# Two-layer attention and gMLP on one Trainium2 core: turning the mixer's operand two tiles ahead and preparing w_out inside the mixer

## The chip, the cores and the metric

The kernel runs on one core of a Trainium2 chip. A core has five engines with queues of their own, each worked through in order: TensorE (PE, whose weight loads have their own row, PEld), VectorE (DVE), ScalarE (ACT), GpSimd (POOL) and SyncE (SP), which here issues every DMA. The metric is the device time of one execution in microseconds, median of several runs.

## The reference

Two layers of attention, each followed by a gated mixer, on 2048 rows of 640 values:

```
x = x + A(layernorm(x));  x = x + B(layernorm(x))      # twice

def B(x, w_in, w_sp, b_sp, w_out):                     # w_in 640 x 1728, w_sp 2048 x 2048, w_out 864 x 640
    z = gelu(x @ w_in)
    z1, z2 = z[..., :864], layernorm(z[..., 864:])
    g = w_sp @ z2 + b_sp[:, None]
    return (z1 * g) @ w_out
```

A is a segmented attention with 32 heads and a compressive memory; the change does not touch it. Every matrix product is done in float16 with each operand split into a high and a low half (x = h + l), in three products: hh, hl and lh.

## The kernel before, in words

Each layer has three stages.

**Attention** (`phase1a`) ends with the projections of row tiles 0 to 11 (x1 = x + o @ wo, stored to DRAM). Tiles 12 to 15 are left to the next stage.

**The mixer** (`phase1b`) goes over the 16 row tiles of 128 rows in the order ts = 0..3, 12..15, 4..11. For each it loads x1 (for tiles 12 to 15 it makes x1 from the attention output `o`, L372 and L375), normalizes it (L303 to L312), splits it into two float16 halves `xnhl` (`split_t`: L318 on ACT, L319 on DVE) and turns it by a transposing DMA into `th` (L320), the stationary operand. Then PE makes the two halves of z = x @ w_in (L395, 30 matmuls each): z2 first, then z1, each followed by a gelu on ACT (L401, L408). z2 is normalized and seven combinations of it are kept as `zb` (L448, L449, L453); z1 goes to DRAM (L409). The half z2 has two accumulators (`zp1`), the half z1 has one (`zp0`). The loop is one tile ahead: in iteration i it loads tile i+2, turns the operand of tile i+1 and multiplies tile i. `th` has two buffers. In the first layer each iteration also advances `other_scales` for w_out by one step (seven loads of 128 rows, a largest value of each, then the scale: L271 to L291), and iterations 7 and 9 store the split w_in (L201, four stores of 1080 KB).

**The spatial stage** (first layer: `phase2f`, second: `phase2s`) multiplies w_sp by z2 in a Strassen-like scheme: eight pairs of row tiles, seven products of 24 matmuls a pair (P1 to P7, L796), whose operands are sums of quarters of w_sp (S1 to S4, made by POOL L781, DVE L784 and L790 and ACT L787 from turned quarters, L760, L764, L773). The gated rows are multiplied by w_out (L876). `SEVEN` is the written order of a pair's steps, with lags in pairs. `PREPARED` lists steps of the first pairs that are put into the mixer: `rows1.0:1` is step rows1 of pair 0, to be issued after the gelu and the normalization of the mixer's tile 1; names without a number come right at the mixer's end.

w_out (`g.wu`, 864 x 640 float32, seven pieces of 128 rows) is split by `staged()` in the first pairs: a piece is loaded to a staging tile (L824), then `split_scaled` makes its two halves on ACT (L90) and DVE (L91), straight into the place that w_in's second half had. After pair 2, `keep()` stores the halves to DRAM (L201, L203: two stores of 960 KB and two of 120 KB); the second layer brings them back from there with `bring()`.

PE's order in the mixer, and that of all engines in the spatial stage, is the program's. The order of the other engines in the mixer is made by a planner, which simulates the engines and hands an instruction to an engine when its inputs are there in that simulation; `issue_after` holds a step until another instruction. Once planned, each queue's order is fixed, and an engine whose next instruction waits does nothing else.

Of the kernel before, what the change touches and what calls it, by code (L numbers as in the profile page):

```python
# [9 lines left out]
F32 = mybir.dt.float32  # L10
# [75 lines left out]
def split_scaled(g, h, l, st, c):  # L86

    nc = g.nc
    iv = g.iv[:st.shape[0], c:c + 1]
    nc.scalar.activation(h, st, AF.Identity, scale=iv)  # L90
    return nc.vector.scalar_tensor_tensor(l, st, iv, h, ALU.mult, ALU.subtract).ins  # L91
# [244 lines left out]
def phase1b(g, o_d, x, x1_d, z1_d, put, after):  # L336
    nc, tc = g.nc, g.tc
    first = not g.wu.made
    with ExitStack() as ctx:
        pool = lambda n, b, **k: ctx.enter_context(tc.tile_pool(name=n, bufs=b, reuse_waits="tile", **k))  # L340
        right = lambda n, b: pool(n, b, side="right")
        if first:
            pool("bp", 1).tile([128, 6 * 1024], F32, name="bp")
            wm = pool("bm", 2)
        pe2, pe1, p2, p1, px2, px1 = right("be2", 2), right("be1", 1), right("b2", 2), right("b1", 1), right("bx2", 2), right("bx1", 3)
        pz1, py, pz0 = pool("bz1", 2, space=PSUM), pool("by", 1, space=PSUM), pool("bz0", 1, space=PSUM)
        ctx.enter_context(tc.manual_schedule(engines=ENGINES))
        wi = [(w.h, w.l) for w in g.wi]
        woh, wol = g.wo.h, g.wo.l

        def load(t):
            if t < NWO:
                x1 = pe2.tile([128, D], F32, tag="x1", name="x1")
                nc.sync.dma_start(x1, x1_d[t])
                return (x1,)
            xt = px2.tile([128, D], F32, tag="xt", name="xt")
            nc.sync.dma_start(xt, x[t])
            o = px1.tile([128, 2, KD, 128], F16, tag="o", name="o")
            d = o_d[t // 4][(t % 4) * 128:(t % 4 + 1) * 128]
            nc.sync.dma_start(o.rearrange("p i k c -> p (i k) c"), d.rearrange("p i c -> p (i c)"), transpose=True)  # L360
            return xt, o[:, 0], o[:, 1]

        def attn_out(t, *a):
            if t < NWO:
                x1 = a[0]
            else:
                xt, oh, ol = a
                yp = py.tile([128, 2, 512], F32, tag="yp", name="yp")
                for k in range(KD):
                    for j, (a, b) in enumerate(((oh, woh), (oh, wol), (ol, woh))):  # L370
                        for n in range(2):
                            nc.tensor.matmul(yp[:, n, :320], a[:, k, :], b[:, k, n * 320:(n + 1) * 320],  # L372
                                             start=(k == 0 and j == 0), stop=(k == KD - 1 and j == 2))
                x1 = pe2.tile([128, D], F32, tag="x1", name="x1")
                nc.vector.scalar_tensor_tensor(x1.rearrange("p (n c) -> p n c", n=2), yp[:, :, :320], g.yw,  # L375
                                               xt.rearrange("p (n c) -> p n c", n=2), ALU.mult, ALU.add)
                nc.sync.dma_start(x1_d[t], x1)
            xn = x1 if t < NWO else xt
            layernorm(g, x1, xn, D, 2, XS)
            return xn  # L380

        def xn_t(xn):
            th = pe2.tile([128, 2, KD, 128], F16, tag="th", name="th")
            hl = pe1.tile([128, 2, D], F16, tag="xnhl", name="xnhl")
            split_t(g, hl, th, xn)
            return th[:, 0], th[:, 1]

        def w_in_half(i, th, tl):
            zp = (pz0, pz1)[i].tile([128, 2, 512], F32, tag=f"zp{i}", name=f"zp{i}")
            wh, wl = wi[i]  # L390
            for k in range(KD):
                for j, (a, b) in enumerate(((th, wh), (th, wl), (tl, wh))):
                    for n in range(2):
                        c = n * FHH
                        nc.tensor.matmul(zp[:, n, :FHH], a[:, k, :], b[:, k, c:c + FHH],  # L395
                                         start=(k == 0 and j == 0), stop=(k == KD - 1 and j == 2))
            return zp

        def z2_half(t, zp):
            z2 = p1.tile([128, FH], F32, tag=f"z2{t % 2}", name="z2")  # L400
            i = nc.scalar.activation(z2.rearrange("p (n c) -> p n c", n=2), zp[:, :, :FHH], AF.Gelu_apprx_tanh, scale=g.zi[1])  # L401
            j = layernorm(g, z2, z2, FH, 2, ZB)
            put(t, z2, p1)
            return i.ins, j.ins

        def z1_half(t, zp):
            z1 = p2.tile([128, FH], F32, tag="z1", name="z1")
            nc.scalar.activation(z1.rearrange("p (n c) -> p n c", n=2), zp[:, :, :FHH], AF.Gelu_apprx_tanh, scale=g.zi[0])  # L408
            return nc.sync.dma_start(z1_d[t], z1).ins  # L409


        g.mark = {}
        ts = [*range(4), *range(NWO, NT), *range(4, NWO)]
        with after(-9):
            a = load(ts[0])
            xn = attn_out(ts[0], *a)
            a = load(ts[1])
            th = xn_t(xn)
        more = other_scales(g, wm, (g.wu,), 6, 0, 0) if first else iter(())
        for i, t in enumerate(ts):  # L420
            late = lambda: ExitStack() if i else after(0)
            b = load(ts[i + 2]) if i + 2 < NT else None
            if i + 1 < NT:
                with late():
                    th1 = xn_t(attn_out(ts[i + 1], *a))
            a = b
            last = z2_half(t, w_in_half(1, *th))
            g.mark[i] = last
            sent = z1_half(t, w_in_half(0, *th))
            th = th1  # L430
            with tc.issue_after(last[1]), tc.issue_after(sent):
                if first and i in (7, 9):
                    g.wi[i == 7].keep()
                for _ in range(1 + (i == 7)):
                    next(more, None)


# [274 lines left out]
""".split()  # L712

PREPARED = """
rows1.0:1 rows0.0:1 max1.0:2 sm1.0:2 max0.0:4 sm0.0:4 hi11.0:5 lo11.0:6 hi22.0:6 lo22.0:6 T11.0:8 T22.0:8 hi21.0:8
lo21.0:8 T21.0:9 rows1.1:9 hi12.0:9 bk22.0:10 bk11.0:10 st11.0:10 lo12.0:10 max1.1:10 rows0.1:11 st22.0:11 bk21.0:12
mS1.0:12 mS3.0:12 mS2.0:13 H2.0:13 max0.1:14 L2.0:14 sm1.1:14 sm0.1:14 H1.0 L1.0 T12.0 hi11.1 st12.0 lo11.1 hi22.1
""".split()


def phase2f(g, w_sp, x1_d, z1_d, zb, out, nxt, rest):
# [93 lines left out]
            held.enter_context(tc.issue_after(i))  # L815
        return held

    def staged():

        w = g.wu  # L820
        for k in range(w.nk):
            n = min(128, w.dram.shape[0] - 128 * k)
            st = nxt.e2.tile([128, D], F32, tag="xt", name="wst")[:n] if k % 2 else nxt.e1.tile([128, D], F32, tag="xh", name="wst")[:n]
            nc.sync.dma_start(st, w.dram[k * 128:k * 128 + n])  # L824
            yield
            split_scaled(g, w.h[:n, k], w.l[:n, k], st, w.c)

    live = {}

    def new(nm, pool, tag, shape, dt=F32):  # L830
# [52 lines left out]
    def item(n, k):  # L883

        a, b = n[:-1], n[-1]
        if a in ("rows", "max", "sm"):
            t = 2 * k + int(b)
            if a == "rows":
                raw[t] = pr.tile([128, S], F32, tag="wr", name="wr")
# [81 lines left out]
    for n, k in ahead:  # L971
        with tc.issue_after(g.mark[NT - 1][n[0] in "Ll"]):
            item(n, k)
    wu = staged()
    for w in range(NP):
        for n, lag in order:
            k = w - lag
            if not 0 <= k < NP or (n, k) in early:
                continue
            with tc.issue_after(g.parted) if w == 0 else ExitStack():  # L980
                item(n, k)
            if (w, n) in ((0, "P1"), (0, "P3"), (0, "P4"), (0, "P5"), (0, "P6"), (0, "P7"), (1, "P1"), (1, "P2")):
                next(wu, None)
            if w + 1 == NP and n in ("P4", "P5", "P6"):
                a = "qkv"[int(n[1]) - 4]
                nc.sync.dma_start(g.wf[a], g.wkept[a])
                if n == "P5":
                    nxt.turned()
        if w == 2:
            g.wu.keep()  # L990
    for w in range(NP, NP + 3):
        for n, lag in order:
            k = w - lag
# [127 lines left out]
class Attention:  # L1121
# [45 lines left out]
    @contextmanager  # L1167
    def after(self, t):

        with self.tc.high_priority(offset=HP2), ExitStack() as held:  # L1170
            for i in self.marks[min(int(1.25 * t) + self.T, max(self.marks))]:
                held.enter_context(self.tc.issue_after(i))
            yield

    def next(self, f):

        if self.now is None:
            f()
        elif self.half is not None:
            self.half.append(f)  # L1180
        else:
            self.post(1, f)
# [798 lines left out]
```

## Time and profile before

| What | Value |
|---|---|
| median of 3 runs | 2202.07 us (2201.21 to 2203.7) |
| the profiled execution | 2203.07 us, of it 2201.3 us span |
| first mixer, from its first z matmul to the first product of the spatial stage | 593.5 to 797.3 us |
| first spatial stage until the next attention's projections begin to mix in | 797.3 to 1134.8 us |
| second mixer | 1669.3 to 1861.0 us |
| PE busy over the span | 2072.4 us (94%) |
| DVE busy | 1624.7 us (74%) |
| ACT, POOL busy | 1218.1 us (55%), 1083.2 us (49%) |

A row of the windows view gives, for a stretch of time, the busy time of each engine with its instructions, then TensorE's granted clock, the mean share of the 16 DMA engines that were busy and what they moved. A row of the waits view says who waited for whom, the total, how many times and the longest. A row of the timeline gives start, duration, engine, line and, in brackets, the idle time before it and what ended it. In the chain of waits a row is a piece of the path that set the end: start, length, what.

### The profile page before, as it was taken

How to read it: one execution, taken by the hardware profiler on the slowest of the kernel's cores; microseconds unless marked ns; L12 is line 12 of the kernel's file. 1: busy time of each engine (PE TensorE's matmuls, PEld its weight loads, DVE VectorE, ACT ScalarE, POOL GpSimd, SP SyncE). 2: the span in 40 equal slices, each digit the busy share in tenths (PEclk: the TensorE clock that was granted, in tenths of full speed). 3: DMA queues.
4: the chain of work that ended last, by engine and by line, in shares of the span. 5: the costliest groups of instructions: out<-in, count | busy, mean ns of one | idle time of the engine just before them, and what ended most of it. 6: DMA issues, size and time to landing. Idle time of an engine off the chain costs nothing.

```text
span 2201.3 us, 48857 instructions
## 1 busy us (share of the span) xinstructions
PE 2072.4 (94%) x19725; PEld 1250.6 (57%) x19725; DVE 1624.7 (74%) x2952; ACT 1218.1 (55%) x1490; POOL 1083.2 (49%) x704
## 2 busy tenths in 40 slices
PE   4889899999899998999999999999999999999999
PEld 2455565666555454555555556566665555555555
DVE  8678888787777788899845887877775686565464
ACT  3499888788633343332323998888874244323221
POOL 2298988888422442344330987788873233000000
PEclk9999999999999999999999999999999999999999
DMA  5626635456757658999676344344567334988885
GB/s 168 184 65 207 157 89 141 109 136 148 208 137 188 170 149 229 236 223 243 181 227 146 95 123 105 106 124 114 138 162 196 102 101 134 276 199 208 226 206 115
DMA packets 514483, 356.16 MB, mean 162 GB/s; under 512 B 409872, under 2 KB 450704, under 8 KB 509136
## 3 DMA queue, kind: packets, MB, share of 16 engines
q1 hardware_dynamic: 514256, 353.04, 61.3%
q8 instruction: 154, 2.52, 0.5%
q14 instruction: 73, 0.60, 0.1%
HBM read 157.44 MB, written 107.43 MB: 120 GB/s over the span
## 4 chain that ended last, share of the span: by engine, by line
PE 66%; DVE 12%; ACT 8%; DMA 5%; issue 5%; POOL 3%; SPq 1%; ACTq 0%; DVEq 0%; POOLq 0%
PE zp L395 12%; PE cyp L594 4%; PE cyp L876 4%; PE vps L1384 3%; PE yps L1416 3%; PE ga L546 3%; PE gb L546 3%; PE pv L1673 3%; ACT P L1620 3%; PE qps L1440 3%; PE mp L1613 3%; PE b L796 3%; PE a L796 2%; PE kps L1440 2%; ACT PHL L1638 2%
## 5 line engine op out<-in xcount | busy, mean ns | idle before, releaser
L1639 POOL TENSOR_TENSOR PHL<-P,PHL 128x1024 f16<-128x1024 f32 x310 | 658.8, 2133 | 184.2 <-ACT PHL L1638 136.6
L1620 ACT ACTIVATE P<-es,sc 128x1024 f32<-128x1024 f32 x320 | 356.1, 1113 | 89.7 <-PE es L1584 87.2
L1630 DVE TENSOR_REDUCE mx<-mp 128x2 f32<-128x1024 f32 (+2 forms) x384 | 321.2, 863 | 85.3 <-PE mp L1584 84.0
L1638 ACT CAST PHL<-P 128x1024 f16<-128x1024 f32 x320 | 333.5, 1042 | 6.3
L395 PEld LDWEIGHTS <-th 128*128 128x128 f16 x1920 | 187.7, 98 | 174.0 <-DMA th<-xnhl 11.8
L796 PEld LDWEIGHTS <-wt 128*128 128x128 f16 x1344 | 131.7, 98 | 124.4 <-DVE wt L790 8.9
L1673 PEld LDWEIGHTS <-PHL 128*128 128x128 f16 x5120 | 167.1, 96 | 56.8 <-DVE oat L1694 19.0
L306 POOL TENSOR_TENSOR lnrs<-lnve,mhalf 128x1 f32<-128x1 f32 x78 | 48.9, 635 | 303.0 <-DVE lnve L305 251.3
L546 PEld LDWEIGHTS <-wt 128*128 128x128 f16 x1344 | 131.2, 98 | 113.0 <-DMA wt<-turned 0.4
L395 PE MATMUL zp<-wi,th 128*128 128x432 f16 x960 | 182.2, 349 | 9.8 <-DMA th<-xnhl 9.7
L1673 PE MATMUL pv<-vs,PHL 128*128 128x41 f16 x5120 | 172.9, 182 | 19.4 <-DVE oat L1694 15.5
L395 PE MATMUL zp<-w,th 128*128 128x432 f16 x960 | 180.4, 347 | 0.0
L1440 PEld LDWEIGHTS <-zb 128*128 128x128 f16 x1200 | 103.1, 99 | 103.0 <-issue 8.5
L781 POOL TENSOR_TENSOR f<-wt 128x1024 f32<-128x1024 f16 x32 | 82.3, 2578 | 139.0 <-DVE wt L790 117.8
L1613 PEld LDWEIGHTS <-qk 64*128 64x128 f16 (+1 forms) x1728 | 65.7, 94 | 127.7 <-issue 94.3
L1613 PE MATMUL mp<-qk 60*128 60x512 f16 (+3 forms) x864 | 108.5, 305 | 18.1 <-DVE mx L1630 12.5
L1416 PE MATMUL yps<-wo,o 128*128 128x320 f16 x720 | 121.0, 305 | 0.0
L1613 PE MATMUL es<-qk 64*128 64x256 f16 (+3 forms) x864 | 106.1, 298 | 9.5 <-ACT P L1620 7.5
L1384 PE MATMUL vps<-zb,w 128*128 128x320 f16 x480 | 83.9, 307 | 4.8 <-DVE phl L1481 4.8
L876 PE MATMUL cyp<-w,ut 128*128 128x320 f16 (+1 forms) x630 | 88.1, 300 | 0.0
L1627 DVE TENSOR_REDUCE mx<-mp 128x4 f32<-128x1024 f32 x64 | 77.8, 1215 | 10.9 <-PE mp L1584 10.8
L1440 PE MATMUL qps<-w,zb 128*128 128x512 f16 x300 | 83.0, 380 | 0.0
(311 smaller groups left out, 4165.6 us busy)
## 6 DMA issues: line engine op xcount, KB each, us to landing
wr<-in_B_w_sp_dram SPq DMA_DIRECT2D x32, 1024.0 KB
qk<-st SPq DMA_DIRECT2D x216, 120.0 KB
z<-z SPq DMA_DIRECT2D x32, 432.0 KB
cz<-z SPq DMA_DIRECT2D x32, 432.0 KB
turned<-wt SPq DMA_DIRECT2D x24, 512.0 KB
wt<-turned SPq DMA_DIRECT2D x24, 512.0 KB
st<-qhl SPq DMA_DIRECT2D x40, 256.0 KB
st<-khl SPq DMA_DIRECT2D x40, 256.0 KB
```

The lines of the kernel that those rows point to most:

```text
L395: nc.tensor.matmul(zp[:, n, :FHH], a[:, k, :], b[:, k, c:c + FHH], start=(k == 0 and j == 0), stop=(k == KD - 1 and j == 2))
L546: nc.tensor.matmul(o[:, :FHH], wt[:, x, m, :], zb[b][:, y, m, :], start=start and i == j == 0, stop=i == NP - 1 and j == 2, skip_group_che ...
L796: nc.tensor.matmul(o[:, :FHH], w[:, x, m, :], zb[b][:, y, m, :], start=start and i == j == 0, stop=i == NP - 1 and j == 2, skip_group_chec ...
L876: nc.tensor.matmul(yp[n][:, :320], a[:kn[k], k, :], b[:kn[k], k, n * 320:(n + 1) * 320], start=(k == 0 and j == 0), stop=(k == KO - 1 and ...
L1416: nc.tensor.matmul(ps, a[:, k, :], b[:, k, c], start=(i == 0), stop=(i == 14))
L1440: nc.tensor.matmul(ps, a[:, k, c], b[:, k, :], start=(i == 0), stop=(i == 14))
L1613: nc.tensor.matmul(out[:, h, o:o + w], a[r, ac], b[r, bc], start=o == 0, stop=False, skip_group_check=True)
L1620: self.last_of["ACT"] = nc.scalar.activation(self.Pf[t], es, AF.Exp, scale=g.esc).ins
L1630: self.last_of["DVE"] = nc.vector.tensor_reduce(mx[:, e, :, i], mp[:, :, o:o + w], AX.X, ALU.max).ins
L1638: nc.scalar.copy(hl[:, 0], P)
L1639: (nc.gpsimd if t < self.T - self.TAIL or t % 2 == 0 else nc.vector).tensor_tensor(hl[:, 1], P, hl[:, 0], ALU.subtract)
L1673: nc.tensor.matmul(pv[:, i, h, 0:PVC - 1], self.P[u][:, x, h, o:o + 128], v[:, j, h0 + h, :], start=first and h == x == 0 and (u, o, i, j) ...
```

## The change

- Both mixers are two tiles ahead. Iteration i loads tile i+3, makes and turns the operand of tile i+2, and multiplies tile i. `th` gets a pool of its own with three buffers (the pool beside x1 had two), 2560 bytes more per partition on the right side of the memory, so that the pools behind it move. The output product of tiles 12 to 15 (L372) comes one tile earlier in PE's order.
- In the first layer's mixer the scale of w_out is advanced by two steps in each of iterations 0 to 3 and by one after (before: one, and two in iteration 7).
- The seven pieces of w_out become steps of `PREPARED`: `wl` loads a piece into one staging tile, `ws` splits it into one pair tile `whl`, `wk` stores the two halves to DRAM (14 stores of 160 KB, the last two of 120 KB). They are placed after mixer tiles 7 to 15. Staging tile and pair tile have one buffer each.
- In pair 0 of the first spatial stage four loads bring w_out's halves from DRAM (`bring()`, at P2, P3, P5, P6); the splitting there and the store after pair 2 are gone.
- Some other steps of `PREPARED` move: lo11.0, max0.1, sm1.1 and sm0.1 by one tile earlier, hi11.1 and lo11.1 from the mixer's end to its tile 14.

```diff
-        pe2, pe1, p2, p1, px2, px1 = right("be2", 2), ...
+        pt3, pe2, pe1, p2, p1, px2, px1 = right("bt3", 3), right("be2", 2), ...
...
-            th = pe2.tile([128, 2, KD, 128], F16, tag="th", name="th")
+            th = pt3.tile([128, 2, KD, 128], F16, tag="th", name="th")
...
             a = load(ts[1])
-            th = xn_t(xn)
+            ths = [xn_t(xn)]
         more = other_scales(g, wm, (g.wu,), 6, 0, 0) if first else iter(())
+        with after(0):
+            b = load(ts[2])
+            ths.append(xn_t(attn_out(ts[1], *a)))
+        a = b
         for i, t in enumerate(ts):
-            late = lambda: ExitStack() if i else after(0)
-            b = load(ts[i + 2]) if i + 2 < NT else None
-            if i + 1 < NT:
-                with late():
-                    th1 = xn_t(attn_out(ts[i + 1], *a))
-            a = b
+            if i + 2 < NT:
+                b = load(ts[i + 3]) if i + 3 < NT else None
+                ths.append(xn_t(attn_out(ts[i + 2], *a)))
+                a = b
+            th = ths.pop(0)
...
-                for _ in range(1 + (i == 7)):
+                for _ in range(1 + (i < 4)):
                     next(more, None)
...
-rows1.0:1 rows0.0:1 max1.0:2 sm1.0:2 max0.0:4 sm0.0:4 hi11.0:5 lo11.0:6 hi22.0:6 lo22.0:6 T11.0:8 T22.0:8 hi21.0:8
-lo21.0:8 T21.0:9 rows1.1:9 hi12.0:9 bk22.0:10 bk11.0:10 st11.0:10 lo12.0:10 max1.1:10 rows0.1:11 st22.0:11 bk21.0:12
-mS1.0:12 mS3.0:12 mS2.0:13 H2.0:13 max0.1:14 L2.0:14 sm1.1:14 sm0.1:14 H1.0 L1.0 T12.0 hi11.1 st12.0 lo11.1 hi22.1
+rows1.0:1 rows0.0:1 max1.0:2 sm1.0:2 max0.0:4 sm0.0:4 hi11.0:5 lo11.0:5 hi22.0:6 lo22.0:6 wl0.0:7 T11.0:8 T22.0:8 ws0.0:8
+hi21.0:8 lo21.0:8 wk0.0:9 wl1.0:9 T21.0:9 rows1.1:9 hi12.0:9 lo12.0:10 ws1.0:9 bk22.0:10 bk11.0:10 st11.0:10 wk1.0:10
+wl2.0:10 ws2.0:10 max1.1:10 rows0.1:11 st22.0:11 wk2.0:11 wl3.0:11 ws3.0:11 bk21.0:12 mS1.0:12 mS3.0:12 wk3.0:12 wl4.0:12
+ws4.0:12 mS2.0:13 H2.0:13 max0.1:13 sm1.1:13 sm0.1:13 wk4.0:13 wl5.0:13 ws5.0:13 L2.0:14 hi11.1:14 lo11.1:14 wk5.0:14
+wl6.0:14 ws6.0:14 wk6.0:15 H1.0 L1.0 T12.0 st12.0 hi22.1
...
+        w = g.wu
+        if a == "wl":
+            n = min(128, w.dram.shape[0] - 128 * int(b))
+            piece[:] = [nxt.e2.tile([128, D], F32, tag="xt", name="wst")[:n], nxt.e1.tile([128, 2, D], F16, tag="xh", name="whl")[:n]]
+            nc.sync.dma_start(piece[0], w.dram[128 * int(b):128 * int(b) + n])
+        elif a == "ws":
+            split_scaled(g, piece[1][:, 0], piece[1][:, 1], piece[0], w.c)
+        elif a == "wk":
+            for i in range(2):
+                nc.sync.dma_start(w.kept[i][:piece[1].shape[0], int(b)], piece[1][:, i])
...
-    wu = staged()
+    wu = g.wu.bring()
+    g.wu.made = True
...
-            if (w, n) in ((0, "P1"), (0, "P3"), (0, "P4"), (0, "P5"), (0, "P6"), (0, "P7"), (1, "P1"), (1, "P2")):
-                next(wu, None)
+            if w == 0 and n in ("P2", "P3", "P5", "P6"):
+                next(wu)
...
-        if w == 2:
-            g.wu.keep()
```

More of the change, by code (lines that the diff above doesn't have):

```diff
@@ L344, in phase1b @@
             wm = pool("bm", 2)
-        pe2, pe1, p2, p1, px2, px1 = right("be2", 2), right("be1", 1), right("b2", 2), right("b1", 1), right("bx2", 2), right("bx1", 3)
+        pt3, pe2, pe1, p2, p1, px2, px1 = right("bt3", 3), right("be2", 2), right("be1", 1), right("b2", 2), right("b1", 1), right("bx2", 2), right("bx1", 3)
         pz1, py, pz0 = pool("bz1", 2, space=PSUM), pool("by", 1, space=PSUM), pool("bz0", 1, space=PSUM)
@@ L429, in phase1b @@
             sent = z1_half(t, w_in_half(0, *th))
-            th = th1
             with tc.issue_after(last[1]), tc.issue_after(sent):
@@ L816, in behind @@
         return held
[L818 to L826, printed above, removed]
+    piece = []
     live = {}
@@ L885, in item @@
         a, b = n[:-1], n[-1]
-        if a in ("rows", "max", "sm"):
+        w = g.wu
[8 more added lines that the diff above has]
+                nc.sync.dma_start(w.kept[i][:piece[1].shape[0], int(b)], piece[1][:, i])
+        elif a in ("rows", "max", "sm"):
             t = 2 * k + int(b)
```

## The prediction

> **What bounds the kernel now.** I read the page first (PE is busy 94% of the span), then the windows around both mixers, then who waited for whom on PE there, then PE's timeline and the chain of waits for each gap, and last DVE's groups. The windows, with PE, PEld, DVE, ACT, POOL, then clock, DMA share and GB/s:
>
> ```profile
> 616.19:698.37 82.18, 82.17 (x480) 46.84 (x480) 61.32 (x111) 28.21 (x41) 21.56 (x24) 1.00 0.48 128
> 698.37:797.26 98.89, 89.82 (x480) 47.19 (x481) 74.96 (x133) 39.01 (x56) 40.10 (x34) 0.98 0.69 169
> 797.26:841.94 44.68, 35.73 (x196) 18.87 (x194) 41.46 (x48) 16.53 (x23) 14.81 (x8) 0.93 0.78 220
> 841.94:884.00 42.06, 42.06 (x242) 24.19 (x243) 36.46 (x54) 13.41 (x16) 15.12 (x7) 0.96 0.83 211
> ```
>
> PE is full in the first half of the first mixer and again from the second pair on. Between, from 698 to 842, it lacks 9.1 us in the mixer and 9.0 us in the first pair. PE's waits from 560 to 860 name the releasers:
>
> ```profile
> PE zp L395 <- DMA th<-xnhl: 9.7, 5, 4.9
> PE c L796 <- DVE wt L790: 7.1, 1, 7.1
> PE c L796 <- DVE u L803: 1.8, 1, 1.8
> ```
>
> PE's timeline has the places; the row at 933 is in a later pair:
>
> ```profile
> 616.19 5.65 PE L395 MATMUL zp<-wi,th 128*128 128x432 f16 x30 [0.59 <-DMA th<-xnhl]
> 700.77 5.65 PE L395 MATMUL zp<-wi,th 128*128 128x432 f16 x30 [2.40 <-DMA th<-xnhl]
> 713.05 5.65 PE L395 MATMUL zp<-wi,th 128*128 128x432 f16 x30 [1.16 <-DMA th<-xnhl]
> 729.10 7.33 PE L395 MATMUL zp<-wi,th 128*128 128x432 f16 x30 [4.92 <-DMA th<-xnhl]
> 775.35 5.65 PE L395 MATMUL zp<-wi,th 128*128 128x432 f16 x30 [0.60 <-DMA th<-xnhl]
> 834.28 0.52 PE L796 MATMUL c<-zb,wt 128*128 128x432 f16 x2 [1.82 <-DVE u L803]
> 841.94 5.99 PE L796 MATMUL c<-zb,wt 128*128 128x432 f16 x22 [7.13 <-DVE wt L790]
> 933.32 4.19 PE L796 MATMUL b<-zb,wt 128*128 128x432 f16 x22 [0.87 <-DVE wt L790]
> ```
>
> So there are two troubles: operands that land late, and DVE, which is late with S1 of the second pair. The gaps also cost clock: 30 matmuls take 7.33 us behind the 4.92 us gap instead of 5.65, and 22 take 5.99 behind the 7.13 us gap where 22 take 4.19 behind 0.87. That is 1.7 and 1.8 us more.
>
> In the second mixer the chain shows ten tiles without a gap. One tile takes 10.95 us, in both:
>
> ```profile
> 1751.49 109.50 PE zp L395 x600
> 631.39 10.95 PE zp L395 x60
> ```
>
> **The operand two tiles ahead.** How long the turning takes, in the chain of waits:
>
> ```profile
> 696.44 4.28 DMA th<-xnhl
> 703.75 9.26 DMA th<-xnhl
> 716.34 12.71 DMA th<-xnhl
> 770.45 4.86 DMA th<-xnhl
> ```
>
> With two buffers an operand can be written only once the tile before the running one is done, so it has one tile, 10.95 us, for normalizing, splitting, waiting in SP's queue and landing. A landing of 12.71 alone is longer. With three buffers it has 21.9 us, which leaves 9.2 us for the rest even at 12.71; DVE's part of it takes 3.2 (groups below). So I take all five waits as gone: 9.67 us (0.59 + 2.40 + 1.16 + 4.92 + 0.60) and 1.7 us of clock, 11.4 us. Bounds: nothing, if SP's order keeps the transposes where they are, and 11.4.
>
> The rest of this edit costs nothing that I see. The loads are the same, one tile earlier. In the second mixer nothing can be gained (ten tiles without a gap). Two rows of the chain and of SP's timeline, at the end of the attention:
>
> ```profile
> 598.67 6.72 DMA o<-ohl
> 605.40 3.07 SPq L360 DMA_TRANSPOSE o<-o  x2
> ```
>
> L372 moves one tile earlier: its matmuls would now start at about 616, and SP issues the first `o` at 605.4, when the attention's last store has landed. Moved pools can wait for other old tiles; the nearest row is this store of 160 KB, for which z1's first gelu waited too. That wait ends at 605.4 and is hidden today because z2 has a second accumulator; unhidden it costs at most 6.7 us, once a mixer. I take 0.
>
> **w_out in the mixer.** Two rows of the chain of waits, the first product with w_out and a load behind the four stores:
>
> ```profile
> 852.31 5.71 PE cyp L876 x42
> 922.12 8.93 DMA cz<-z
> ```
>
> Out of the first pairs go seven loads of 320 KB or less, seven L90 on ACT and seven L91 on DVE; four loads with the same 2.21 MB (864 x 640 in two float16 halves) come in, needed only by the first w_out product, now at 852 us. Out of pair 2 go the four stores, another 2.21 MB; they go into the mixer as 14. So DMA moves 2.21 MB more in all. The windows by stage:
>
> ```profile
> 690.00:740.00 50.00, 41.52 (x217) 21.35 (x216) 30.86 (x62) 17.34 (x25) 13.37 (x14) 0.97 1.03 243
> 740.00:797.00 57.00, 56.40 (x310) 30.03 (x309) 50.06 (x86) 23.80 (x34) 28.44 (x23) 1.00 0.44 109
> 797.00:842.00 45.00, 36.05 (x198) 19.02 (x196) 41.78 (x49) 16.85 (x23) 15.07 (x8) 0.93 0.78 221
> 842.00:962.00 120.00, 119.13 (x707) 69.48 (x708) 107.32 (x148) 37.88 (x42) 49.06 (x26) 0.98 0.91 229
> ```
>
> Loads and stores of w_out, 4.4 MB, are some 20 us of DMA at 221 GB/s; the stretch 740 to 797 has 32 us free, 690 to 740 has none. After 842 the stores' 10 us of 109 go, and with them the wait at 933 (0.87), which a load of z1 behind these stores made (8.93 us from issue to landing).
>
> The rest is DVE's account up to the row at 841.94, whose S1 is made at the end of DVE's queue for the first pair. DVE was busy 74.96 + 41.46 = 116.4 us of the 143.6 from 698.37 on, idle 27.2. Its groups in 690 to 842:
>
> ```profile
> L303 DVE BATCH_NORM_STATS2 lnst<-z 128x6 f32<-128x432 f32 x18 | 10.1, 600 | 16.7 <-ACT z L401 16.7
> L312 DVE TENSOR_SCALAR x<-x,lnmv,lnrs 128x640 f32<-128x640 f32 x8 | 9.4, 1176 | 0.1
> L319 DVE TENSOR_TENSOR xnhl<-x,xnhl 128x640 f16<-128x640 f32 x8 | 8.4, 1046 | 2.1 <-ACT xnhl L318 2.1
> L312 DVE TENSOR_SCALAR z<-z,lnmv,lnrs 128x864 f32<-128x864 f32 x9 | 6.6, 729 | 5.1 <-POOL lnrs L306 5.1
> L91 DVE SCALAR_TENSOR_TENSOR w<-wst,iv,w 128x640 f16<-128x640 f32 x5 | 6.3, 1251 | 2.9 <-ACT w L90 2.9
> L303 DVE BATCH_NORM_STATS2 lnst<-x 128x6 f32<-128x320 f32 x14 | 6.1, 475 | 0.0
> L279 DVE TENSOR_REDUCE wap<-wmst 128x1 f32<-128x640 f32 (+1 forms) x2 | 1.6, 815 | 1.3 <-DMA wmst<-in_B_w_out_dram 1.3
> ```
>
> The five L91 stay in the stretch, and the two that ran after 842 join them: + 1.7 at 0.87 each (timeline below). The last two L279 go ahead of it: - 1.6. One tile's preparation goes ahead too (L303 twice 0.475, L312 1.18, L319 1.05): - 3.2. That leaves 113.3 us of work. Of the idle time, PE's own gaps made 10.8 (9.1 + 1.7, within the 16.7 that DVE waited for the gelu), ACT's L90 2.9 and the last L279 1.3; 12.2 stays. S1 is then ready at 698.4 + 113.3 + 12.2 = 823.9. PE gets there at 841.94 - 10.8 - 8.95 = 822.2. The wait would shrink from 8.95 to 1.7 us.
>
> This asks DVE to be packed well, and L91 has two prices:
>
> ```profile
> 808.70 0.88 DVE L91 SCALAR_TENSOR_TENSOR w<-wst,iv,w 128x640 f16<-128x640 f32 x1 [0.95 <-ACT w L90]
> 818.24 2.73 DVE L91 SCALAR_TENSOR_TENSOR w<-wst,iv,w 128x640 f16<-128x640 f32 x1
> 817.21 3.09 POOL L781 TENSOR_TENSOR f<-wt 128x1024 f32<-128x1024 f16 x1 [1.16 <-DVE wt L790]
> ```
>
> The long one ran wholly beside a POOL instruction. In 740 to 797 POOL is busy 28.4 of 57 us, in 797 to 842 15.1 of 45, so the moved steps meet it in half of the cases: seven at a mean of 1.8 us are 12.6 instead of the 8.0 counted above (6.3 + 1.7), 4.6 more. The wait left is then 1.7 to 6.3; I take 5, above the middle, since a queue fixed in advance is never packed to the last microsecond, and a clock loss of 0.6 behind it. Gain here: 8.95 + 1.8 - 5.6 = 5.2, bounds 0 (PE comes sooner and waits longer) and 10.75.
>
> [...]
>
> **The sum.** 11.4 + 5.2 + 0.9 (pair 2) = 17.5. For the 2.21 MB more, in a mixer whose DMA is already full until 740, I take off 1.5 us (between 0 and the 10 us that they last). 2203.07 (its span 2201.3 and 1.8 around it) - 16.0 = 2187.1; the median of the runs is 1.0 below the profiled execution, so 2186. That is a gain of 0.7%; a measurement of this kernel tells 0.2%, 4.4 us, from no change.
>
> [...]
>
> **The rivals.**
>
> *The wait only moves.* Operands come in time, but DVE has no room: S1 of the second pair comes as late as now less what PE's gaps cost DVE, or less. For it: 50.1 of 57 us busy in 740 to 797, before seven more steps are put there. Against it: the 27 us of idle time. Gain 11.4 + 0.9 at most, with L91's 4.6 and the DMA's 1.5 lost again 6: 2196 to 2190, say 2194.
>
> *The order of the queues eats it.* SP, ACT and DVE are ordered anew by the planner in both mixers; the transposes stand behind loads of pieces that wait for a staging tile, or z1's gelu behind an old tile. No change: 2202.
>
> *ACT stands still for a piece (slower).* Piece tiles have one buffer: `ws` waits on ACT until its load has landed and until the store of the piece before has been read. Behind it on ACT stand the gelus, and z1's accumulator has no second buffer, so PE stops when ACT is held for longer than one half, 5.5 us. The trace has such a wait:
>
> ```profile
> 825.37 0.83 ACT L90 ACTIVATE w<-wst,iv 128x640 f16<-128x640 f32 x1 [9.72 <-DMA wst<-in_B_w_out_dram]
> ```
>
> At 9.72 each, seven pieces cost 7 x 4.2 = 29 us, at 12.71 (the slowest landing) 50; against the gain of 17.5 that gives 2202 + 12 = 2214 at the lower price. It decides from 8 us of landing a piece on. Against it: it is the only such wait of the seven L90 today, and from 740 on, where most pieces lie, DMA has room; the four pieces or so placed before find it full.
>
> **How the numbers follow.** The forecast 0.56 (its own range 2179, with all of both waits gone, to 2191), the moved wait 0.20, no gain 0.09, ACT held 0.15. Faster by over 0.2% are the first two: 0.76; same 0.09; slower 0.15. The range goes from 2179 to 2206: it takes in the first three and the mildest of the fourth.
>
> **What would show it.** Right: no `th` row among PE's waits in 600 to 800; the first product of the spatial stage at about 786 instead of 797.3; the second c product waiting under 6 us; no L201 store near 917; no L90 wait for a load over 5 us. Wrong: gelus (L401, L408) behind a `ws` with PE waiting for ACT; `th` landings over 20 us; a new wait of PE for w_out at the first tail; gaps in the second mixer, which has none.

## The result and the profile after

| What | Before | After |
|---|---|---|
| median of the runs | 2202.89 us (4 runs, 2201.21 to 2204.9) | 2214.05 us (4 runs, 2212.35 to 2216.51) |
| ratio after to before | | 1.0051, 95% interval 1.0034 to 1.0069 |
| the profiled execution's span | 2201.3 us | 2212.2 us |

The changed kernel is slower by 0.5%. The forecast was 2186, in a range from 2179 to 2206, so a gain of 0.7% was expected and a loss came. The first mixer and the first pairs came out nearly as worked out. Apart from 3 us ahead of the first mixer, which the experiments below cannot tell from the scatter between executions, the loss is in the second layer.

The windows of the first mixer and the first pair (columns as in the prediction):

```profile
616.19:698.37 82.18, 82.18 (x483) 47.06 (x481) 63.76 (x120) 28.54 (x41) 23.35 (x24) 1.00 0.62 153
698.37:788.03 89.66, 89.66 (x493) 48.04 (x491) 79.51 (x134) 44.08 (x63) 42.27 (x35) 1.00 0.75 220
788.03:834.00 45.97, 42.01 (x215) 21.67 (x214) 39.14 (x49) 17.45 (x22) 14.63 (x8) 0.93 0.94 243
```

PE has no gap left in the mixer. From 698.37 to the first product it takes 89.7 us, where it took 98.9 (this kernel's mixer began 3 us later, so it had a little more left to do). DVE does more in less time (79.5 us busy of 89.7; before 75.0 of 98.9). Who waited for whom on PE, first from 600 to 900 us (one row is all there is), then the first two rows from 1600 us to the end:

```profile
PE c L800 <- DVE wt L794: 4.0, 1, 4.0
```

```profile
PE zp L395 <- DVE lnve L305: 16.6, 1, 16.6
PE gc L548 <- DMA wt<-wn: 5.5, 1, 5.5
```

The five `th` rows are gone and the wait for S1 has shrunk, but two waits have appeared that the profile of before did not have. PE's timeline gives the places of all three waits, and what they cost in clock:

```profile
827.56 6.97 PE L800 MATMUL c<-zb,wt 128*128 128x432 f16 x22 [3.96 <-DVE wt L794]
1670.69 8.41 PE L395 MATMUL zp<-wi,th 128*128 128x432 f16 x30 [16.62 <-DVE lnve L305]
1875.05 5.86 PE L548 MATMUL gc<-zb,wt 128*128 128x432 f16 x24 [5.54 <-DMA wt<-wn]
```

The second row stands ahead of the second mixer's first z matmul: 30 matmuls in 8.41 us where the next 30 take 5.64, so 16.6 + 2.8. The third stands at the start of the second spatial stage: 24 in 5.86 where the next 24 take 4.54, so 5.5 + 1.3. Cutting both profiles at the same five starts of PE (first z matmul, first product, first `vps` of the second attention, second mixer's first z matmul, first `gc`) gives an account that closes:

| Stretch | Before | After | Difference |
|---|---|---|---|
| start to the first z matmul | 593.54 | 596.51 | +2.97 |
| first mixer | 203.72 | 191.52 | -12.20 |
| first product to first `vps` | 361.70 | 356.49 | -5.21 |
| `vps` to the second mixer's first z | 510.37 | 526.17 | +15.80 |
| second mixer, to the first `gc` | 196.05 | 204.36 | +8.31 |
| `gc` to the end | 335.92 | 337.15 | +1.23 |
| span | 2201.3 | 2212.2 | +10.9 |

**Where the 16.6 us come from.** ACT's timeline, the split of the second mixer's first tile, after and before:

```profile
1662.90 0.73 ACT L318 CAST xnhl<-x 128x640 f16<-128x640 f32 x1 [5.25 <-DMA o<-ohl]
```

```profile
1644.55 0.73 ACT L318 CAST xnhl<-x 128x640 f16<-128x640 f32 x1 [1.49 <-DVE x L312]
```

The split runs 18 us later than before, though this kernel was by then some 14 us ahead and PE was free for the tile from 1654.07 on (1670.69 - 16.62). SP's timeline shows the attention's last stores, and the operand's transpose behind them:

```profile
1654.10 0.33 SPq L500 DMA_DIRECT2D wr<-in_B_w_sp_dram  x1
1654.53 0.38 SPq L1428 DMA_DIRECT2D x<-xt  x1
1657.68 1.86 SPq L1714 DMA_DIRECT2D o<-ohl  x2
...
1666.19 1.38 SPq L320 DMA_TRANSPOSE th<-xnhl  x1
```

The releaser in a row is inferred, and here it names a neighbour (so does PE's row at 1670.69, whose L305 belongs to the next tile: PE waited for the transpose, and the weight loads, PEld, have 16.7 us of waiting for `th` there). In the compiled program the split waits for no store of `ohl`, but for six other DMAs; the last of them in SP's order is the store at 1654.53: x1 of row tile 11, out of the attention's tile `xt`, issued right behind 1024 KB of w_sp's rows. It waits because the two tiles now share memory. The addresses in the compiled programs (bytes in a partition):

```
                         before            after
xt (attention's last)    178432-180992     178432-180992
xnhl (second mixer)      182368-184928     179808-182368
z2 (second mixer, even)  163360-166816     160800-164256
wn (spatial, 2nd buffer) 157056-161152     157056-161152
```

The new pool for `th` has pushed the pools behind it down by 2560 bytes, and `xnhl` has come to lie 1184 bytes deep in `xt`.

**Where the 5.5 us come from.** The same shift puts z2, which is used until the mixer's end, 352 bytes deep into `wn`, the split of S1 and S2 for the second spatial stage. The rows of the tile `wn`, first after, then before, give the first and the last start:

```profile
L527 ACT CAST wn<-s x2: 1041/1042/1042, 1868.3 to 1869.2; 128x1024 f16<-128x1024 f32 x2
```

```profile
L525 ACT CAST wn<-s x2: 1035/1036/1036, 1785.3 to 1807.2; 128x1024 f16<-128x1024 f32 x2
```

They ran in the middle of the mixer, and now run at its end; the transposes follow, and the third product waits for one of them. The first of the two splits, whose own buffer lies lower and under no late tile, is late as well: the planner has put both side by side in ACT's order, behind the mixer's last `zb`. Why it put the first one there, the addresses alone do not say.

### The profile page after: what moved, and what is told of

Same layout as the page of the kernel before. It is cut to its first block, busy times and chain, and to the rows that moved or that the text cites. A ratio compares the mean times of both kernels' runs of the same rounds, so it can differ in the third digit from the quotient of the medians.

```text
span 2212.2 us, 48897 instructions
## 1 busy us (share of the span) xinstructions
PE 2075.9 (94%) x19725; PEld 1252.5 (57%) x19725; DVE 1626.2 (74%) x2952; ACT 1221.0 (55%) x1490; POOL 1084.3 (49%) x704
## 4 chain that ended last, share of the span: by engine, by line
PE 69%; DVE 9%; ACT 9%; issue 5%; DMA 5%; POOL 3%; SPq 1%; POOLq 0%; ACTq 0%; DVEq 0%
PE zp L395 16%; PE cyp L596 4%; PE cyp L871 4%; ACT P L1624 3%; PE gb L548 3%; PE pv L1677 3%; PE yps L1420 3%; PE ga L548 3%; PE vps L1388 3%; PE qps L1444 3%; PE a L800 3%; PE b L800 3%; PE mp L1617 3%; ACT PHL L1642 2%; PE kps L1444 2%
## 5 line engine op out<-in xcount | busy, mean ns | idle before, releaser
L395 PEld LDWEIGHTS <-th 128*128 128x128 f16 x1920 | 188.6, 98 | 180.2 <-DMA th<-xnhl 16.7
L395 PE MATMUL zp<-wi,th 128*128 128x432 f16 x960 | 183.2, 350 | 16.6 <-DVE lnve L305 16.6
L764 ACT ACTIVATE wn<-wr,wiv 128x1024 f16<-128x1024 f32 x32 | 36.6, 1145 | 90.4 <-DVE wiv L752 40.3
```

## The experiments

Two theories. **Memory**: 2560 bytes make tiles share memory with others that come free late. **Order**: the loop two tiles ahead orders the second layer's queues anew, whatever the addresses. Differences below are from the kernel before, run beside on the same chip.

**The shift without the change.**

```diff
+        if not first:
+            right("bt", 1).tile([128, D], F32, name="bt")
         pe2, pe1, p2, p1, px2, px1 = right("be2", 2), ...
```

> The kernel before, with one unused tile of 2560 bytes per partition put in front of the right-hand pools in the second mixer only; nothing else changes. Two theories of the loss in the second layer. Memory: the changed kernel lost there because its pools lie 2560 bytes lower, so xnhl comes to lie over a tile of the attention's last output (free only after its store) and the spatial stage's wn over z2 of the mixer (free only at the mixer's end). Then this kernel must show both losses with the order of before: a wait of PE for the second mixer's first operand of 13 to 17 us (with clock 16 to 19), and a wait at the second spatial stage's start of 5 to 6 (with clock 6 to 7): 2203 + 22 to 26 = 2225 to 2229. Order: the two-ahead loop put the queues of the second layer in another order, and addresses do not matter: 2203, and neither wait.

Measured: 2231.5 against 2205.49 us, ratio 1.0122 (1.0104 to 1.0141). PE's waits from 1600 us on:

```profile
PE zp L397 <- DMA th<-xnhl: 15.7, 1, 15.7
PE gc L548 <- DMA wt<-wn: 5.6, 1, 5.6
```

An unused tile in the old kernel brings both waits, and 26 us. The order that the loop two tiles ahead makes is out as their cause, for this kernel does not have it. The time lies 2.5 us above the expected range, as does the kernel before in these runs (2205.49 where 2203 was put in).

**The shift by other sizes.** The same edit with 864 and with 2208 bytes.

> The kernel before with an unused tile of 864 bytes in front of the second mixer's right-hand pools instead of 2560. By the addresses of the compiled program, xnhl then begins at 181504, above the attention's xt tiles (which end at 180992), and z2 at 162496, above the end of wn (161152). Memory theory, with the overlap itself as the cause: neither wait, 2203. If any shift disturbs the plan: 2210 to 2230.

> The same with 2208 bytes: xnhl begins at 180160, 832 bytes inside the last xt tile, and z2 at 161152, just above the end of wn. Memory theory: the wait for the second mixer's first operand is there (about 16 us and 2 to 3 of clock), the wait at the second spatial stage is not: 2203 + 18 to 20 = 2221 to 2223. If the second wait hangs on the mixer being late and not on the 352 bytes, it is there too: 2228 to 2231.

Measured: 864 bytes, 2205.01 against 2205.66, ratio 0.9997 (0.9988 to 1.0006), and neither wait. 2208 bytes: 2222.52, ratio 1.0075 (1.0063 to 1.0087). Its wait for the operand, and its first `gc`, which has no wait although the mixer began 16.6 us later than in the profile of before:

```profile
PE zp L397 <- DMA th<-xnhl: 15.5, 1, 15.5
```

```profile
1883.85 4.54 PE L548 MATMUL gc<-zb,wt 128*128 128x432 f16 x24
```

So it is not the shift that costs but what it overlaps: 864 bytes overlap nothing that is busy, 2208 reach `xt` alone, 2560 reach `wn` too. The first wait is worth 17 us here, and the second, by difference from the 26, 9.

**Two ahead in both mixers, at other addresses.** The second mixer's third `th` buffer is put behind `xnhl`; then w_sp's third row buffer, which is not used in the mixer, is put above `s` and `wn`.

```diff
+        if first:
+            pt = [right("bt3", 3)] * 3
+            pe2, pe1 = right("be2", 2), right("be1", 1)
+        else:
+            pe2, pe1 = right("be2", 2), right("be1", 1)
+            pt = [pe2, pe2, right("bt1", 1)]
...
+            th = pt[next(nth) % 3].tile([128, 2, KD, 128], F16, tag="th", name="th")
...
-        pr, ps, ph = pool("dr", 3), pool("ds", 2), pool("dh", 2)
+        pr, ps, ph, pr1 = pool("dr", 2), pool("ds", 2), pool("dh", 2), pool("dr1", 1)
```

The first kernel has all but the last two lines.

> The changed kernel, with the second mixer's third th buffer in a pool of its own behind x1 and xnhl, so that th, x1 and xnhl have their addresses of before; z1, z2 and all behind them still lie 2560 bytes lower. The loop is two ahead as in the changed kernel. Memory: the wait for the first operand goes (16.6 and 2.8 of clock), the wait of 5.5 at the second spatial stage stays: 2214 - 19 = 2195, between 2192 and 2199. Order: both waits stay, 2214.

> As the kernel with the third buffer behind xnhl, and in the second spatial stage the third buffer of w_sp's rows, which no step uses before the mixer's end, is put above the pools of s and wn, so that wn ends 8192 bytes lower and no longer reaches z2. Two ahead in both mixers. Memory: both waits go: 2214 - 19.4 - 6.9 = 2188, between 2184 and 2192. Order: 2214.

Measured: 2196.28, ratio 0.9963 (0.9951 to 0.9976), with the second wait alone; and 2189.8, ratio 0.9935 (0.9922 to 0.9947), with neither. The second mixer's first z matmul and the first `gc`, in the one and in the other:

```profile
1656.38 5.63 PE L402 MATMUL zp<-wi,th 128*128 128x432 f16 x30
1857.94 6.91 PE L555 MATMUL gc<-zb,wt 128*128 128x432 f16 x24 [5.52 <-DMA wt<-wn]
```

```profile
1657.84 5.63 PE L402 MATMUL zp<-wi,th 128*128 128x432 f16 x30
1853.92 4.54 PE L556 MATMUL gc<-zb,wt 128*128 128x432 f16 x24
```

The splits into `wn` start at 1851.2 us in the one, at the mixer's end, and at 1773.8 in the other, in its middle. The loop is two ahead in both kernels and the waits go with the addresses: memory explains the loss in the second layer.

**The second mixer as it was.** One ahead, two `th` buffers, old pools; the first layer as changed.

```diff
+        pt3 = right("bt3", 3) if first else None
...
+            th = (pt3 or pe2).tile([128, 2, KD, 128], F16, tag="th", name="th")
...
+        n = 2 if first else 1
```

> The changed kernel with the second mixer as before (one ahead, two th buffers, old pools). Memory and order both expect the losses of the second layer to go and the gain of the first to stay: 2186 to 2190. If it stays above 2195, the second layer's loss comes from something that the first layer hands on.

Measured: 2190.76, ratio 0.9932 (0.9920 to 0.9945). The second mixer takes 196.12 us to the first `gc`, as with two ahead at the other addresses (196.08) and as before (196.05): there two ahead brings nothing. The time is that of the kernel with two ahead at the other addresses (0.9935), and just above the 2186 to 2190 expected.

**Each edit alone**, in the first layer. The first kernel is the one above with w_out staged, split and kept as before and `PREPARED` as before; the second is the changed kernel with the mixer's loop and pools of before:

```diff
-        pt3, pe2, pe1, p2, p1, px2, px1 = right("bt3", 3), right("be2", 2), ...
+        pe2, pe1, p2, p1, px2, px1 = right("be2", 2), ...
...
+            b = load(ts[i + 2]) if i + 2 < NT else None
```

> The kernel before with the first change alone, in the first mixer alone: th in a pool of three, two tiles ahead; w_out is split in the spatial stage as before, and the second mixer is as before. By the prediction's account the five th waits go with their clock (-11.4), and the second pair's S1 waits as before or less: 2203 - 11.4, and up to 3 lost again because the third tile's normalization now runs in the attention's tail: 2192 to 2195. If PE only comes sooner to an S1 that DVE cannot deliver earlier, the c wait grows from 9 to 17 to 20 us and the time is 2200 to 2203.

> The kernel before with the second change alone: w_out scaled, split and stored by steps in the first mixer and loaded in the first pair; both mixers one tile ahead with two th buffers. If the two edits add up, this one is worth the rest: the c wait falls from 9 to 4 or 5, five th waits stay near 9.7: 2197 to 2200. If the added 2.2 MB and splits in the mixer lengthen the landings of th, the th waits grow past 15 us and the time is 2203 to 2210: then this edit needs the other.

Measured: two ahead alone 2200.7, ratio 0.9976 (0.9966 to 0.9986); w_out alone 2202.19, ratio 0.9987 (0.9975 to 0.9998). By the ratios that is 5 and 3 us of 2206, where both together (the kernel above, 0.9932) give 15. Both expectations missed. (Single executions scatter: the kernel before and the three with an unused tile of 2560, 864 and 2208 bytes have the same first layer, and take 203.7, 203.7, 206.3 and 205.6 us in its mixer.) PE's waits, 480 to 1000 us, of two ahead alone and then of w_out alone:

```profile
PE c L802 <- DVE wt L796: 7.1, 1, 7.1
PE zp L396 <- ACT z L409: 4.1, 1, 4.1
...
PE c L802 <- DVE u L809: 2.0, 1, 2.0
```

```profile
PE zp L395 <- DMA th<-xnhl: 12.8, 5, 4.5
...
PE c L798 <- DVE wt L792: 4.3, 1, 4.3
```

| Stretch | Before | Two ahead | w_out | Both |
|---|---|---|---|---|
| first mixer | 203.72 | 198.33 | 208.38 | 191.50 |
| first product to `vps` | 361.70 | 361.21 | 355.77 | 356.64 |

w_out alone gains its 6 us behind the mixer (the wait for S1 falls from 9.0 to 4.3) and loses 4.7 in it: the operands come later (12.8 us of waits for 9.7, and 3.2 us of clock for 1.7). With two ahead as well, the mixer shows neither. Two ahead alone gains 5.4 in the mixer, not 11.4, because a new wait has come. ACT's timeline there:

```profile
729.33 0.72 ACT L318 CAST xnhl<-x 128x640 f16<-128x640 f32 x1 [7.66 <-DMA th<-xnhl]
729.96 0.97 ACT L409 ACTIVATE z<-zp,sc 128x864 f32<-128x864 f32 x1
```

PE stands 4.1 us for that gelu and then takes 8.21 us for 30 matmuls, 2.6 more than the 5.64 of other rows. `xnhl` has one buffer. The next split waits until the transposing DMA has read the last one, and the gelu of z1, for which PE has one accumulator, stands behind it. That is one suspect. The other is the scale of w_out, whose last steps run on DVE at 741 to 750 us, beside a busy POOL (21.5 us of the 50 from 700 on); the changed kernel has them earlier. Three kernels take away the one, the other and both; the second buffer is one of the two `xt` tiles, free by then, for every second split from the tenth tile on:

```diff
+            if first and n > 8 and n % 2:
+                hl = px2.tile([128, 2, D], F16, tag="xt", name="xnhl")
```

```diff
-                for _ in range(1 + (i == 7)):
+                for _ in range(1 + (i < 4)):
```

> The kernel with two ahead in the first mixer alone (w_out as before), and from the tenth tile of that mixer on every second split goes into a buffer of its own (one of the two xt tiles, free by then), so that ACT need not wait until the transposing DMA has read the one xnhl tile. If that wait (7.66 us on ACT, with the gelu of z1 behind it, PE 4.1 us and 2.6 of clock) is what the first edit turned the th waits into, PE's wait for that gelu goes: 2200.7 - 6.7 = 2194, between 2192 and 2197. If the gelu is late for another reason: 2200.

> The kernel with two ahead in the first mixer alone (w_out split in the spatial stage as before), with the scale of w_out advanced as in the changed kernel: two steps in each of iterations 0 to 3 instead of in iteration 7. If the late scale steps (their loads of 320 KB among the slow transposes, and L290 to L83 on DVE at 741 to 750 behind POOL) are what makes z1's gelu late when the operand comes two tiles ahead, the wait of 4.1 us goes and the first mixer takes 191 to 193 us instead of 198.3: 2194 to 2196 beside 2206 for the kernel before. If the one xnhl tile alone is the cause, the mixer stays at 196 to 199 and the time at 2200.

> The same with the second buffer for every second split from the tenth tile on. If the two causes together are all that keeps PE waiting in the mixer, no wait for the gelu is left and the mixer takes 191.5 to 192 us instead of 194.3: 2194 to 2196. If another step of the first pair's preparation is the cause, a wait of 2 to 3 us stays and the time is 2198.

| Two ahead alone, and with | first mixer | wait for the gelu | ratio to before |
|---|---|---|---|
| nothing more | 198.33 | 4.1 | 0.9976 (0.9966 to 0.9986) |
| a second buffer for the split | 194.34 | 2.7 | 0.9963 (0.9951 to 0.9975) |
| the scale earlier | 193.74 | 1.9 | 0.9965 (0.9953 to 0.9977) |
| both | 192.49 | 0.6 | 0.9948 (0.9935 to 0.9961) |

The medians are 2200.7, 2198.76, 2197.8 and 2193.99. With the second buffer the gelu is late 25 us further on, behind DVE; with the scale earlier it is late at the old place, by less; with both next to nothing is left:

```profile
755.16 5.63 PE L401 MATMUL zp<-w,th 128*128 128x432 f16 x30 [2.68 <-ACT z L414]
```

```profile
733.71 5.63 PE L396 MATMUL zp<-w,th 128*128 128x432 f16 x30 [1.61 <-ACT z L409]
```

```profile
731.47 5.63 PE L401 MATMUL zp<-w,th 128*128 128x432 f16 x30 [0.56 <-ACT z L414]
```

So both suspects add to the wait, and together they are the missing part: with both taken away the edit alone is worth 0.52%, 11.5 us, near the 11.4 of the account. This rests on the two ends: the intervals of neighbouring rows overlap, and each of the two middle kernels came out between the two values that it was expected at. How the scale's steps reach the gelu at the old place, through their loads or through DVE, is not shown. Why the changed kernel's mixer has no gap with one `xnhl` buffer was not tried; there the split waits for the DMA at one place in 690 to 830 us, for 0.4 us.

**The attention's tail.** The changed kernel loads the third tile in the part that the planner puts first, so its normalization gets between the attention's last steps on DVE. Two kernels, with the first layer alone changed, put the load back; the second holds the normalization too.

```diff
             with after(0):
-                b = load(ts[2])
                 ths.append(xn_t(attn_out(ts[1], *a)))
-            a = b
+            a = load(ts[2])
```

> The kernel with two ahead in the first mixer alone (and w_out in the mixer), with the load of the third tile taken out of the part that the planner puts first in the attention's tail. If that early load, by which the third tile's normalization gets onto DVE between the attention's last products, makes the first z matmul 3 us later (596.5 against 593.5), it comes back to 593.5 to 594.5 and the time falls by 2 to 3 us, to 2188; otherwise 2191 and the first z matmul at 596.5.

> As the kernel with the load taken out, and the third tile's normalization and split held besides until the attention's last steps. By the same reason 2187 to 2189, first z matmul at 593.5 to 594.5, if the load alone was not enough; if the third tile is now late for PE, a th wait at about 615 and 2190 or more.

Measured: 2190.06, ratio 0.9922 (0.9908 to 0.9936), first z matmul at 598.89; and 2187.75, ratio 0.9916 (0.9901 to 0.9932), at 595.76. The intervals overlap with that of the kernel that they start from (0.9932), and the first z matmul did not go back to 593.5. One execution each cannot decide it: the kernels with 864 and 2208 unused bytes, whose first layer is that of before, have that matmul at 595.66 and 595.51, and two ahead alone and its kernel with the second buffer run the same instructions in the same order up to that matmul, and have it at 595.45 and at 599.14. The +2.97 us of the account are within that. Whether the early load costs anything stays open.

The kernel with the held third tile has the lowest median, 0.84% below the kernel before, but its interval overlaps with those of the other good ones.

## Why the prediction was wrong

**The operand two tiles ahead, -11.4: right in size, in part by luck.** The mixer is 12.2 us shorter, all five waits and their clock are gone. But the time left for a landing was not all that counts. By itself the edit gave 5.4, because the one `xnhl` tile and the late scale steps put the wait on ACT; the other edit moves the scale, which the prediction did not give as a reason.

**w_out and S1, -5.2 and -0.9: near in the sum.** From the first product to `vps` 5.21 us went, forecast 6.1. The wait that is left is 3.96, forecast 5; its clock is 2.8 (6.97 us for 22 matmuls that take 4.19), forecast 0.6, a term that no row of before gives. The two errors offset each other in part. L91's price was bounded well:

```profile
L91 DVE SCALAR_TENSOR_TENSOR whl<-wst,iv,whl 128x640 f16<-128x640 f32 x6 | 8.6, 1432 | 1.3 <-ACT whl L90 1.3
```

1.43 us each, between 0.88 and 1.8. (The long L91 of the prediction did not run wholly beside a POOL instruction: POOL's ended at 820.30, L91 0.67 us later.) The stall at 933 us is gone.

**The DMA, +1.5: not seen.** With both edits in, the first mixer is without a gap. Without two ahead it is 4.7 us longer, with 12.8 us of waits for operands where the kernel before has 9.7. Whether longer landings make those operands late, or steps of DVE ahead of them, was not separated.

**The step that failed** is the one on the moved pools: "Moved pools can wait for other old tiles; the nearest row is this store of 160 KB", "unhidden it costs at most 6.7 us, once a mixer. I take 0." The question was asked and priced by how long one store lasts. What counts is when the old tile comes free against when the new one was written before (1662.90 against 1644.55) and against when PE is free for it (1654.07). The store that held it back was another one, of x1, issued at 1654.53 behind w_sp's rows. And it was put once a mixer, while a second tile, `wn`, was not looked at, though it belongs to the next stage and takes the mixer's memory from below. The two cost 19.4 and 6.9 us (waits and clock) where 0 stood; with the tiles at other addresses the two-ahead kernel gives 2189.8, within the range. "In the second mixer nothing can be gained" held, so there the edit had only its price. The prediction named "gaps in the second mixer, which has none" as a sign of error; what came is close to that, gaps at its two ends. Its signs of being right are all in the first layer, and there they came: no `th` row, the first product at 788.0 for 786, no L90 wait over 5 us.

**The rivals.** ACT standing still for a piece was forecast at 2214, the time that was measured, but that is a coincidence, for its mechanism did not occur: the longest wait of an L90 for its load is 4.1 us, below the 8 from which it decides, and PE never waited for it. "The wait only moves" describes two ahead alone, with ACT in the place where it had DVE. A gain eaten by the order of the queues did not show: the second layer's loss went with the addresses, in the new order.

## What to carry to other kernels

A pool that grows moves every pool stacked behind it, in every stage that shares the code: before pricing such an edit, list which old tiles the moved ones come to lie over, when those are released, and how early the new ones were written until now; here 352 bytes of overlap with a tile in use to the end of a stage moved work that was done ahead to that end. Give a deeper buffer only to the stage that waits, or stack the added buffer where its neighbours are idle. For an operand made further ahead, look at every tile on its way: the wait can move to one that is less deep (here 7.66 us on ACT for the one `xnhl`). Two edits that clear each other's waits are judged together (5 and 3 us alone, 15 both).

## What was unexpected of the hardware

**A small DVE instruction took 2.07 us beside POOL.** In the kernel with the split's second buffer, from DVE's and then POOL's timeline, and all executions of the line (least, median and most in ns):

```profile
747.17 2.07 DVE L80 TENSOR_TENSOR pw<-pw,floor 128x1 f32<-128x1 f32 x1
```

```profile
741.71 7.51 POOL L792 TENSOR_TENSOR f<-wt 128x1024 f32<-128x1024 f16 x3 [2.87 <-DVE pw L290]
```

```profile
L80 DVE TENSOR_TENSOR pw<-pw,floor x7: 150/160/2074, 20.9 to 747.2; 128x1 f32<-128x1 f32 x7
```

One value per partition took 2.07 us, where its median is 0.16, and ended at 749.24; the last of POOL's three ended at 749.22. In the kernel before and in the changed one it took 2.07 and 2.08 us once each, also beside POOL. What ties the two together is not shown.

**Behind the longer waits of PE the clock cost 1.3 to 2.9 us, and the length of the wait did not order it.** Nothing is lost in the rows behind waits of 1.61, 2.40 and 2.68 us (5.63 to 5.65 us for 30 matmuls). In rows of 21 to 30 matmuls of 128x432 behind waits of 3.87 us and more it is 1.3 to 2.9 us, in no order: 1.6 behind 3.87, 2.8 behind 3.96, 2.9 behind 4.02, 1.7 behind 4.34, 1.7 behind 4.92, 1.3 and 2.4 behind 5.5 (5.86 and 6.91 for 4.54), 1.4 behind 15.72, 2.8 behind 16.62. In the changed kernel's three rows, behind 16.62, 3.96 and 5.54, the granted clock fell to 0.50 within the wait and was back at 1.00 at 1676.3, 833.2 and 1877.7 us, which is 5.7, 5.7 and 2.7 us into the row. Half of these times is 2.8, 2.8 and 1.3 us, close to what the rows lost. What sets how long the clock stays at 0.50 is not shown.
